# PSUM banks of the seven FFN2 products from other tiles, two partial sums moved to the q and k tiles, and a higher rank for the relu chain of the last pass

## The chip, the core and the metric

One core of a Trainium2 chip runs the whole program. The metric is the device time in microseconds of one execution. Three executions of the kernel before took 696.64, 698.77 and 699.04 us; the median is 698.77 us. A profiled execution, from which every duration below is read, took 701.44 us.

## The reference

Three layers follow each other, all in float32, on 4 x 576 = 2304 tokens of width 512:

```
s = (q @ k.T) / 8, masked to the 64 keys that end at the query      # 8 heads of 64
x = softmax(s) @ v                                                  # 2304 x 512
h = maximum(x @ w_in, 0)                                            # 512 -> 2048   (FFN1)
x = (h * h) @ w_out                                                 # 2048 -> 512
h = x @ w2_in                                                       # 512 -> 1024   (FFN2)
solu = h * softmax(h)
ln = (solu - mean) / sqrt(var + 1e-6) * g_ln
out = ln @ w2_out                                                   # 1024 -> 512
```

The weights arrive as float64 bit patterns and are turned into float32 on the core. FFN1 and FFN2 are computed with each operand split into a high part (the matrix engine's rounded float32) and a rest, in three products per pair of operands (`TERMS`).

## The kernel before

**A planner sets the order.** The kernel doesn't issue instructions directly. It calls `add(engine, us, rank, function, after, take, give, port)` for every step, with an estimated duration, a rank and the slots (buffers, PSUM banks) that the step takes and gives back. `Plan.run` then picks, again and again, the step that can start first by its own estimates (the lower rank wins a tie) and in the end emits all steps in the order of their planned starts. The order on each engine is thus fixed before the program runs; waits between engines are semaphores that the framework derives from who writes and reads which tile. `port=True` makes the planner keep a VectorE step and a GpSimd step from being planned at the same time; nothing on the chip enforces it.

**FFN1** runs in five passes of 8, 6, 8, 6 and 8 blocks of 64 tokens (`ffn`, 512 or 384 columns). In a pass each of 16 weight chunks `kk` takes 12 matrix products into a `ps_h` bank (L538), then the chain relu on ScalarE (L544), square on ScalarE (L548, the high part `g`), exact square on GpSimd (L551), rest on VectorE (L554), then 12 products into `ps_y` (L567). Attention for the next pass (`attention`, units of two blocks) is ranked between; `attention_of(t)` spreads its units over the pass before.

**The conversion of w2** (`assembled`, `operands`, `weights`) is ranked into the last pass: each 128x512 weight block is loaded, scaled on ScalarE (L219), completed by three VectorE steps (L223, L228, L233), and split into high part (ScalarE) and rest (VectorE: L278 for w2_in, L254 for w2_out). L286 forms differences of w2_in blocks.

**FFN2** treats two tiles of 128 tokens at a time (`pair2`, nine pairs, n = 0 to 8). Its 2x2 block product is done with seven products instead of eight; each is 6 matrix instructions of 512 columns (L735), into four banks called a, b, c and d. In order: A11 into a, S2 into b, S3 into d, S1 into c, then A12 added to a, A22 added to d, S4 added to c. Between them ScalarE and VectorE take the sums out: `p1` = a (L741, `keep1`), `u2` = b + p1 (L745), `u3` = d + u2 (L749), c22 = c + u3 (L760), c11 = a (L757), c21 = d + u2 (L763), c12 = c + u2 (L766). Banks a and b are two tiles of `ps_a`; banks c and d are the two halves of one two-bank tile of `ps_b`. `p1`, `u2` and `u3` are `wm` buffers, which the weight conversion uses too.

**Behind each pair** (`behind`, once per tile): maximum (L807), exp, solu (L818), centring, squares, transposes into `ps_t` (L835), high part on ScalarE (L841) and rest on VectorE (L845) of the transposed rows, 24 products with w2_out into a `ps_a` bank (L852), scaling and store.

Of the kernel before, what the change touches and what calls it, by code (L numbers as in the profile page):

```python
# [8 lines left out]
F32 = mybir.dt.float32  # L9
# [9 lines left out]
P = 128  # L19
# [5 lines left out]
class Plan:  # L25
# [14 lines left out]
    def add(self, eng, us, rank, fn, after=(), take=(), give=(), port=False, late=0.0, at=0.0):  # L40
        t = dict(eng=eng, us=us, rank=rank, fn=fn, after=[a for a in after if a], take=take, give=give, port=port, late=late, at=at,
                 start=None, n=len(self.tasks))
        self.tasks.append(t)
        return t
# [52 lines left out]
def kernel(  # L97
# [20 lines left out]
    NT, DM = out.shape  # L118
# [12 lines left out]
    HALF, LAST = len(FIRSTS), len(PASSES) - 1  # L131
# [9 lines left out]
    ps_b = ctx.enter_context(tc.tile_pool(name="ps_b", bufs=2, space=PSUM))  # L141
# [42 lines left out]
    with ExitStack() as c1:  # L184
# [344 lines left out]
        def ffn(t, n0, n1, kk, rank, done):  # L529
# [41 lines left out]
            in_of[t, kk] = i  # L571
            if kk == KF - 1:
                x_free.setdefault(t, []).append(i)
            r = add("ACT", N / 1200 + 0.11, rank, relu, [i], take=["r"], give=["a"])
            s = add("ACT", N / 1200 + 0.11, rank, square, [r], take=["g"])
            e = add("POOL", N / 600 + 0.19, rank, exact, [s], port=True)
            e = add("DVE", N / 960 + 0.07, rank, rest, [e], port=True, give=["r"])
            first = kk == 0 and n0 == 0

            before = [p for k, p in out_of.items() if k[0] == t and (last or k[1:3] == (0, 0))]  # L580
# [27 lines left out]
        CHUNKS = (16.27, 26.54, 25.57)  # L608
        V0, LATER, OUT = 3.12, 52.7, 4.55
        LEAD = 14.41  # L610
        UNIT = (1.68, 2.12, 15.1, 22.97)
        for n, (kind, kk) in enumerate((kind, kk) for kk in range(KF) for kind in "ab"):
            weights(kind, kk, LOADS[n] if n < len(LOADS) else PAIR0 + PAIR * n / 2 - 2)
# [6 lines left out]
            attention(n, rank)  # L620

        def attention_of(t):
            lo = begin[t - 1] + LATER * (t == 1)
            hi = begin[t] - 10
            n = PASSES[t] // 2
            for i in range(n):
                attention(starts[t] // 2 + i, lo + i * (hi - lo) / n)
# [47 lines left out]
        def term(name):  # L675
            return raw_p.tile([P, 512], F32, tag="wm", name=name, bufs=WMB)

        ring = {}
        phase_of = {}
        M6, TURN = 6 * (512 / 2400 + 0.0135), 0.95  # L680

        def pair2(n, rank, rank_o):
# [39 lines left out]
            WHERE = {"A11": (0, 0), "A12": (0, 1), "A22": (1, 0), "S1": (2, 0), "S2": (2, 1), "S3": (3, 0), "S4": (3, 1)}  # L722

            def product(bank, x, w, begins, ends):
                if begins and bank in "ab":
                    o[bank] = ps_a.tile([P, 512], F32, tag="a", name="ps_h2")
                elif begins and "c" not in o:
                    ps = ps_b.tile([P, 2, 512], F32, tag="b", name="ps_h2")
                    o["c"], o["d"] = ps[:, 0], ps[:, 1]
                k, half = WHERE[x]  # L730
                m = 0
                for r in range(2):
                    for wi, xi in TERMS:
                        at = half * 256 + r * P
                        T.matmul(o[bank], o["xx", k][:, xi, at : at + P], w2i[w, r][:, wi, :], start=begins and m == 0,  # L735
                                 stop=m == 5, skip_group_check=True)
                        m += 1

            def keep1():
                o["p1"] = term("p1")  # L740
                S.activation(out=o["p1"], in_=o["a"], func=AF.Copy)  # L741

            def u2():
                o["u2"] = term("u2")
                V.tensor_tensor(out=o["u2"], in0=o["b"], in1=o["p1"], op=ALU.add)  # L745

            def u3():
# [30 lines left out]
            def pe(k, bank, x, w, begins, after, **kw):  # L778
                return add("PE", M6, rank + 0.01 * k, lambda: product(bank, x, w, begins, True), [*xs_, ready[w, 0], ready[w, 1], *after], **kw)

            soon = rank - 30
            p1 = pe(0, "a", "A11", "B11", True, [], take=["a"])
            e1 = add("ACT", 0.60, soon, keep1, [p1], take=["wm"])
            p6 = pe(1, "b", "S2", "T2", True, [p1], take=["a"])
            e2 = add("DVE", 0.68, soon, u2, [p6, e1], take=["wm"], give=["a", "wm"])
            p7 = pe(2, "d", "S3", "T3", True, [p6], take=["b"])
            e3 = add("DVE", 0.68, soon, u3, [p7, e2], take=["wm"])
            p5 = pe(3, "c", "S1", "T1", True, [p7])
            f22 = add("DVE", 0.68, soon, c22, [p5, e3], take=["wb"], give=["wm"])
            p2 = pe(4, "a", "A12", "B21", False, [p5, e1])  # L790
            f11 = add("ACT", 0.60, soon, c11, [p2], take=["wb"], give=["a"])
            p4 = pe(5, "d", "A22", "T4", False, [p2, e3])
            f21 = add("DVE", 0.68, soon, c21, [p4, f22])
            p3 = pe(6, "c", "S4", "B22", False, [p4, f22], give=["wb"] * 4)
            f12 = add("DVE", 0.68, soon, c12, [p3, f11, f21], give=["b", "wm"])
            phase_of[n] = [p3]

            for k, (i, _, _) in enumerate(tiles):
                behind(k, i, o, rank + LATE0 * (n == 0), rank_o + k * 2 * mm(512), [f11, f12] if k == 0 else [f21, f22])
# [1 line left out]
        def behind(k, i, p, rank, rank_o, done):  # L801
# [62 lines left out]
            a = add("DVE", 1.95, rank, solu, [a])  # L864
            a = add("ACT", 1.10, rank, centered, [a])
            r = add("ACT", 1.25, rank + 3, squares, [a], give=["wb"])
            p_ = add("PE", TURN, rank_o - 8, transposes2, [a], take=["t", "t"])
            r = add("POOL", 2.0, rank, root, [r, p_], give=["wb"])
            ls = []
            for hf in range(2):  # L870
# [17 lines left out]
        o = {}  # L888
# [57 lines left out]
```

## Time and profile before

| what | us |
|---|---|
| median of three executions | 698.77 |
| profiled execution, whole | 701.44 |
| its span, first to last instruction | 699.6 |
| TensorE busy in the span | 682.5 |
| VectorE busy | 391.2 |
| ScalarE busy | 358.9 |
| GpSimd busy | 132.3 |

The page counts as TensorE busy also the time in which a product runs at the lower clock, so that 98% is not 98% of the work rate. A 12-product step of 512 columns shows a length of 2.88 us in the timeline and the next one starts 2.72 us after it: products overlap by their drain, and the distance of starts is what one costs. In the timelines below an instruction line ends in square brackets where the engine was idle before it, with the length of that idle time and what ended it.

### The profile page before, as it was taken

To read this page: it belongs to the slowest core of one execution; us is meant where nothing else is said; L and a number is where in the kernel's file an instruction comes from. 1 tells how busy PE (TensorE), PEld (TensorE's weight loads), DVE (VectorE), ACT (ScalarE), POOL (GpSimd) and SP (SyncE) were. 2 spreads that over 40 slices of the span, in tenths; PEclk is the share of its full clock that TensorE was granted. 3 is DMA by queue.
4 is the path that set the end of the run, shared out by engine and by line. 5 is a ranking of instruction groups with operands and counts; after the bars stand their busy time and mean duration, and the time that the engine had idled before them with its cause. 6 is when DMAs were issued, how large, how long until landed. Compare 5 with 4: busy or idle time off the path is not lost.

```text
span 699.6 us, 11257 instructions
## 1 busy us (share of the span) xinstructions
PE 682.5 (98%) x4377; PEld 576.3 (82%) x4377; DVE 391.2 (56%) x737; ACT 358.9 (51%) x831; POOL 132.3 (19%) x160
## 2 busy tenths in 40 slices
PE   8999999999999999999999999989999999999997
PEld 4678778899998888888999988877778888888885
DVE  4989989633423222114333126997985577656551
ACT  5876775624445242425444234664874466445652
POOL 1023231412323121213232112320210000000000
PEclk8999999999999999999999999999999999999999
DMA  7774656051222111103110103333021110110001
GB/s 249 231 244 142 219 192 221 4 166 54 69 69 83 33 66 35 34 2 128 54 53 31 46 31 129 112 120 121 0 91 61 60 61 31 42 49 31 30 16 45
DMA packets 33253, 60.50 MB, mean 86 GB/s; under 512 B 2992, under 2 KB 14768, under 8 KB 33200
## 3 DMA queue, kind: packets, MB, share of 16 engines
q1 hardware_dynamic: 32656, 59.52, 26.0%
q8 instruction: 34, 0.56, 0.3%
q10 hardware_dynamic: 544, 0.26, 0.1%
q14 instruction: 19, 0.16, 0.1%
HBM read 50.34 MB, written 9.44 MB: 85 GB/s over the span
## 4 chain that ended last, share of the span: by engine, by line
PE 77%; DVE 12%; ACT 4%; DMA 3%; issue 2%; SPq 1%; ACTq 0%; DVEq 0%
PE ps_y L567 24%; PE ps_h L538 21%; PE ps_o L852 13%; PE ps_h L735 10%; PE ps_v L450 2%; PE ps_s L380 2%; PE ps_lt L835 2%; PE ps_p L423 2%; ACT e L395 1%; DMA wraw<-in_w_out 1%; DVE wm L233 1%; DVE wm L228 1%; PE ps_warm L893 1%; DVE g L554 1%; DVE nmax L807 1%
## 5 line engine op out<-in xcount | busy, mean ns | idle before, releaser
L567 PE MATMUL ps_y<-g,wb 128*128 128x512 f32 (+2 forms) x1008 | 214.3, 365 | 4.0 <-DVE g L554 3.9
L538 PE MATMUL ps_h<-x,wa 128*128 128x512 f32 (+2 forms) x1008 | 209.3, 361 | 1.9 <-ACT r L544 1.2
L567 PEld LDWEIGHTS ps_y<-g,wb 128*128 128x128 f32 x1008 | 177.3, 189 | 29.1 <-DVE g L554 6.2
L538 PEld LDWEIGHTS ps_h<-x,wa 128*128 128x128 f32 x1008 | 177.1, 188 | 24.2 <-ACT r L544 1.5
L551 POOL TENSOR_TENSOR r<-r 128x512 f32<-128x512 f32 (+2 forms) x84 | 83.7, 997 | 302.4 <-ACT g L548 270.6
L554 DVE TENSOR_TENSOR g<-r,g 128x512 fp32r<-128x512 f32 (+2 forms) x84 | 56.4, 673 | 130.4 <-POOL r L551 130.4
L544 ACT ACTIVATE r<-ps_h 128x512 f32<-128x512 f32 (+2 forms) x84 | 44.8, 534 | 119.8 <-PE ps_h L538 113.9
L852 PE MATMUL ps_o<-w2o,lnT 128*128 128x512 f32 x432 | 101.2, 393 | 0.7 <-ACT lnT L841 0.4
L852 PEld LDWEIGHTS ps_o<-w2o,lnT 128*128 128x128 f32 x432 | 80.3, 188 | 17.8 <-ACT lnT L841 0.7
L395 ACT ACTIVATE e<-e,nmax 128x128 f32<-128x128 f32 x112 | 43.4, 391 | 31.6 <-DVE nmax L388 31.6
L735 PE MATMUL ps_h<-w2i,xx 128*128 128x512 f32 x189 | 53.3, 390 | 0.0
L548 ACT ACTIVATE g<-r 128x512 fp32r<-128x512 f32 (+2 forms) x84 | 47.7, 569 | 7.6 <-PE ps_y L567 5.7
L405 POOL TENSOR_TENSOR e<-e,sums 128x512 f32<-128x512 f32 x28 | 31.0, 1107 | 69.3 <-DVE sums L401 68.9
L735 PEld LDWEIGHTS ps_h<-w2i,xx 128*128 128x128 f32 x189 | 35.5, 188 | 7.6
L812 ACT ACTIVATE e<-h,nmax 128x1024 f32<-128x1024 f32 x18 | 20.7, 1150 | 34.2 <-DVE nmax L807 34.2
L829 POOL TENSOR_SCALAR rstd<-rstd 128x1 f32<-128x1 f32 x18 | 4.3, 241 | 169.5 <-ACT h L826 168.9
L219 ACT ACTIVATE wm<-wraw 128x512 f32<-128x512 f32 x47 | 31.4, 672 | 7.4 <-DMA wraw<-in_w_in 4.7
L233 DVE SCALAR_TENSOR_TENSOR wm<-wraw,wm 128x512 int32<-128x512 int32 x48 | 34.2, 716 | 0.1
L228 DVE SCALAR_TENSOR_TENSOR wm<-wraw,wm 128x512 int32<-128x512 int32 x48 | 33.4, 700 | 0.1
L383 DVE SCALAR_TENSOR_TENSOR e<-ps_s,mask 128x512 f32<-128x512 f32 x28 | 18.1, 683 | 24.4 <-PE ps_s L380 24.4
L845 DVE TENSOR_TENSOR lnT<-ps_lt,lnT 128x512 fp32r<-128x512 f32 x36 | 23.1, 683 | 14.0 <-ACT lnT L841 14.0
L463 DVE TENSOR_TENSOR x<-ps_v,x 128x512 fp32r<-128x512 f32 (+1 forms) x20 | 12.7, 636 | 24.6 <-ACT x L460 24.6
(102 smaller groups left out, 743.7 us busy)
## 6 DMA issues: line engine op xcount, KB each, us to landing
wraw<-in_w_in SPq DMA_DIRECT2D x24, 512.0 KB, 3.6
wraw<-in_w_out SPq DMA_DIRECT2D x24, 512.0 KB, 4.0
vt<-in_v SPq DMA_DIRECT2D x32, 256.0 KB, 3.0
kt<-in_k SPq DMA_DIRECT2D x16, 384.0 KB, 3.7
xr<-x_dram SPq DMA_DIRECT2D x18, 256.0 KB, 3.4
out<-o SPq DMA_DIRECT2D x18, 256.0 KB, 2.0
qt<-in_q SPq DMA_DIRECT2D x16, 256.0 KB, 2.8
x_dram<-y SPq DMA_DIRECT2D x12, 256.0 KB, 2.7
```

The costliest lines, as they stand in the source:

```text
L219: S.activation(out=o["m"], in_=o["raw"][:, :, 1].bitcast(F32), func=AF.Copy, scale=REBIAS)
L228: V.scalar_tensor_tensor(out=t, in0=o["raw"][:, :, 1], scalar=-0x80000000, in1=t, op0=ALU.bitwise_and, op1=ALU.bitwise_or)
L233: V.scalar_tensor_tensor(out=t, in0=o["raw"][:, :, 0], scalar=29, in1=t, op0=ALU.logical_shift_right, op1=ALU.bitwise_or)
L395: S.activation(out=o["er"][:, a, w], in_=s, func=AF.Exp, scale=SCALE if begins else 1.0, bias=o["nmax"][:, a, w : w + 1], accum_out=o["sum ...
L538: T.matmul(ps[:, :N], wa[kk][:, wi, c * P : c * P + P], xs[t][:, xi, c, n0:n1], start=n == 0, stop=n == 3 * DC - 1)
L544: S.activation(out=o["r"], in_=o["h"][:, :N], func=AF.Relu)
L548: S.activation(out=o["g"][:, 0, :N], in_=o["r"], func=AF.Square)
L551: G.tensor_tensor(out=o["r"], in0=o["r"], in1=o["r"], op=ALU.mult)
L554: V.tensor_tensor(out=o["g"][:, 1, :N], in0=o["r"], in1=o["g"][:, 0, :N].bitcast(F32), op=ALU.subtract)
L567: T.matmul(acc[t][d][:, n0:n1], wb[kk][:, wi, d * P : d * P + P], o["g"][:, xi, :N], start=kk == 0 and n == 0 and n0 == 0, stop=last and n ...
L735: T.matmul(o[bank], o["xx", k][:, xi, at : at + P], w2i[w, r][:, wi, :], start=begins and m == 0, stop=m == 5, skip_group_check=True)
L852: T.matmul(o["o"], o["l", hf][:, xi, kk % 4, :], w2o[kk][:, wi, :], start=kk == 0 and n == 0, stop=kk == KF2 - 1 and n == 2)
```

## The change

It has five parts.

1. In `pair2`, banks a and d now come together, and banks b and c. For pairs 0 and 1 a and d are two tiles of `ps_a`, and c and b are the halves of one `ps_b` tile that is kept from pair 0 on (`kept[0]`). From pair 2 on a and d are the halves of a second kept `ps_b` tile. The same two tiles serve all later pairs.
2. `p1` and `u2` are no longer `wm` buffers: they use the SBUF space of attention's q and k tiles, one buffer each, so that they wait for the last attention unit and for the evictions of the pair before.
3. In the last pass of FFN1 the relu chain (relu, square, exact, rest) gets a rank that is 60 lower, and `exact` is no longer planned under the port rule but 0.4 us longer.
4. Attention for passes 2 to 4 starts 4 us later in the plan (`lo`).
5. The transposes of the last two tiles are ranked 24 instead of 8 ahead of their products.

```diff
-            r = add("ACT", N / 1200 + 0.11, rank, relu, [i], take=["r"], give=["a"])
-            s = add("ACT", N / 1200 + 0.11, rank, square, [r], take=["g"])
-            e = add("POOL", N / 600 + 0.19, rank, exact, [s], port=True)
-            e = add("DVE", N / 960 + 0.07, rank, rest, [e], port=True, give=["r"])
+            soon = rank - SOON * (t == LAST)
+            r = add("ACT", N / 1200 + 0.11, soon, relu, [i], take=["r"], give=["a"])
+            s = add("ACT", N / 1200 + 0.11, soon, square, [r], take=["g"])
+            e = add("POOL", N / 600 + 0.19 + 0.4 * (t == LAST), soon, exact, [s], port=t != LAST)
+            e = add("DVE", N / 960 + 0.07, soon, rest, [e], port=True, give=["r"])
...
+        SOON = 60
...
-            lo = begin[t - 1] + LATER * (t == 1)
+            lo = begin[t - 1] + (LATER if t == 1 else 4)
...
-                if begins and bank in "ab":
+                if begins and n < 2 and bank in "ad":
                     o[bank] = ps_a.tile([P, 512], F32, tag="a", name="ps_h2")
-                elif begins and "c" not in o:
-                    ps = ps_b.tile([P, 2, 512], F32, tag="b", name="ps_h2")
-                    o["c"], o["d"] = ps[:, 0], ps[:, 1]
+                elif begins and bank not in o:
+                    if n in (0, 2):
+                        kept.append(ps_b.tile([P, 2, 512], F32, tag="b", name="ps_h2"))
+                    o.update(c=kept[0][:, 0], b=kept[0][:, 1])
+                    if n > 1:
+                        o.update(a=kept[1][:, 0], d=kept[1][:, 1])
...
-                o["p1"] = term("p1")
+                o["p1"] = at_p.tile([P, 512], F32, tag="q", name="p1", bufs=1)
...
-                o["u2"] = term("u2")
+                o["u2"] = at_p.tile([P, 512], F32, tag="k", name="u2", bufs=1)
...
+            p1 = pe(0, "a", "A11", "B11", True, free if n > 1 else [], take=["a"] if n < 2 else ["b"] * (n == 2))
+            e1 = add("ACT", 0.60, soon, keep1, [p1, *gone_by, *free])
+            p6 = pe(1, "b", "S2", "T2", True, [p1, *free], take=["b"] * (n == 0))
+            e2 = add("DVE", 0.68, soon, u2, [p6, e1, *gone_by, *free])
+            p7 = pe(2, "d", "S3", "T3", True, [p6, *free], take=["a"] * (n < 2))
...
-            p_ = add("PE", TURN, rank_o - 8, transposes2, [a], take=["t", "t"])
+            p_ = add("PE", TURN, rank_o - (8 if i < NT // P - 2 else 24), transposes2, [a], take=["t", "t"])
```

Where it moves instructions, first on TensorE where the last pass of FFN1 meets pair 0 (`ps_h` with a number is a bank of the seven products, `x24` are two steps in a row). Before, the last FFN1 steps and the first products of the pair:

```order
L567 MATMUL ps_y<-g,wb 128x512 x24
L538 MATMUL ps_h<-x,wa 128x512 x12
L567 MATMUL ps_y<-g,wb 128x512 x12
L538 MATMUL ps_h<-x,wa 128x512 x12
L735 MATMUL ps_h_4654<-w2x,xx 128x512 x3
L735 MATMUL ps_h_4654<-w2i,xx 128x512 x3
L567 MATMUL ps_y<-g,wb 128x512 x12
L735 MATMUL ps_h_4700<-w2v,xx 128x512 x3
L735 MATMUL ps_h_4700<-w2i,xx 128x512 x3
L567 MATMUL ps_y<-g,wb 128x512 x12
```

Now:

```order
L567 MATMUL ps_y<-g,wb 128x512 x12
L538 MATMUL ps_h<-x,wa 128x512 x12
L567 MATMUL ps_y<-g,wb 128x512 x12
L538 MATMUL ps_h<-x,wa 128x512 x12
L567 MATMUL ps_y<-g,wb 128x512 x12
L538 MATMUL ps_h<-x,wa 128x512 x12
L567 MATMUL ps_y<-g,wb 128x512 x12
L742 MATMUL ps_h_4724<-w2x,xx 128x512 x3
L742 MATMUL ps_h_4724<-w2i,xx 128x512 x3
L742 MATMUL ps_h_4736<-w2v,xx 128x512 x3
```

The products of pair 0, which stood between the last three steps into `ps_y`, now follow in one piece behind a strict alternation of L538 and L567; its first two products go to 4724 and 4736, and the third and fourth to 4748 and 4736.

On VectorE in the last pass (`wm` are the conversion's buffers, L554 is the end of the relu chain). Before, up to the 13th L554 of the 16 in this pass:

```order
L286 TENSOR_TENSOR wm<-wm 128x512
L278 TENSOR_TENSOR w2i<-wm,w2i 128x512
L223 TENSOR_SCALAR wm<-wm 128x512
L278 TENSOR_TENSOR w2i<-wm,w2i 128x512 x2
L228 SCALAR_TENSOR_TENSOR wm<-wraw,wm 128x512
L223 TENSOR_SCALAR wm<-wm 128x512
L233 SCALAR_TENSOR_TENSOR wm<-wraw,wm 128x512
L228 SCALAR_TENSOR_TENSOR wm<-wraw,wm 128x512
L554 TENSOR_TENSOR g<-r,g 128x512
L233 SCALAR_TENSOR_TENSOR wm<-wraw,wm 128x512
L254 TENSOR_TENSOR w2o<-wm,w2o 128x512 x2
L554 TENSOR_TENSOR g<-r,g 128x512
```

Now, up to the same one:

```order
L278 TENSOR_TENSOR w2i<-wm,w2i 128x512
L286 TENSOR_TENSOR wm<-wm 128x512
L278 TENSOR_TENSOR w2i<-wm,w2i 128x512
L286 TENSOR_TENSOR wm<-wm 128x512
L278 TENSOR_TENSOR w2i<-wm,w2i 128x512
L286 TENSOR_TENSOR wm<-wm 128x512
L554 TENSOR_TENSOR g<-r,g 128x512
L278 TENSOR_TENSOR w2i<-wm,w2i 128x512 x3
L223 TENSOR_SCALAR wm<-wm 128x512 x2
L228 SCALAR_TENSOR_TENSOR wm<-wraw,wm 128x512 x2
L233 SCALAR_TENSOR_TENSOR wm<-wraw,wm 128x512 x2
L554 TENSOR_TENSOR g<-r,g 128x512
```

The 13th L554 now stands ahead of the first w2_out steps (L254), and the 12th ahead of the last three splits of w2_in (L278).

On TensorE in pair 3, the last four of its seven products (the later pairs go the same way). Before:

```order
L735 MATMUL ps_h_5383<-w2e,xx 128x512 x3
L735 MATMUL ps_h_5383<-w2i,xx 128x512 x3
L735 MATMUL ps_h_5360<-w2x,xx 128x512 x3
L735 MATMUL ps_h_5360<-w2i,xx 128x512 x3
L735 MATMUL ps_h_5383<-w2p,xx 128x512 x3
L735 MATMUL ps_h_5383<-w2i,xx 128x512 x3
L735 MATMUL ps_h_5383<-w2x,xx 128x512 x3
L735 MATMUL ps_h_5383<-w2i,xx 128x512 x3
```

Now:

```order
L742 MATMUL ps_h_4736<-w2e,xx 128x512 x3
L742 MATMUL ps_h_4736<-w2i,xx 128x512 x3
L742 MATMUL ps_h_5105<-w2x,xx 128x512 x3
L742 MATMUL ps_h_5105<-w2i,xx 128x512 x3
L742 MATMUL ps_h_5105<-w2p,xx 128x512 x3
L742 MATMUL ps_h_5105<-w2i,xx 128x512 x3
L742 MATMUL ps_h_4736<-w2x,xx 128x512 x3
L742 MATMUL ps_h_4736<-w2i,xx 128x512 x3
```

The order of the products is the same; S1 and S4 (w2e and the last w2x) write one tile, A12 and A22 (the first w2x and w2p) the other, where before S1, A22 and S4 all wrote tile 5383.

## Rows read from the trace of the kernel before

**Rows 1.** The page: engines, busy us, share of the span, instructions.

```profile
PE 682.5 (98%) x4377; PEld 576.3 (82%) x4377; DVE 391.2 (56%) x737; ACT 358.9 (51%) x831; POOL 132.3 (19%) x160
```

**Rows 2.** Busy time by stretch; columns PE, PEld, DVE, ACT, POOL, clock, DMA, GB/s.

```profile
426.11:470.49 44.38, 42.54 (x185) 34.82 (x184) 41.77 (x65) 27.83 (x49) 10.92 (x8) 0.98 0.39 122
...
465.00:470.00 5.00, 3.16 (x12) 2.22 (x11) 4.15 (x9) 3.88 (x7) 0.00 (x0) 0.88 0.40 115
...
470.00:475.00 5.00, 5.00 (x19) 4.00 (x18) 3.67 (x6) 1.49 (x3) 1.04 (x1) 0.77 0.29 95
```

**Rows 3.** Who TensorE waited for: total us, times, longest.

```profile
PE ps_y L567 <- DVE g L554: 3.9, 4, 1.8
...
PE ps_h L735 <- DVE h L760: 1.8, 5, 1.2
```

**Rows 4.** TensorE in order of time, 432 to 532 us: start, us, instruction, idle before.

```profile
434.37 2.88 PE L567 MATMUL ps_y<-g,wb 128*128 128x512 f32 x12
...
464.29 0.84 PE L735 MATMUL ps_h<-w2x,xx 128*128 128x512 f32 x3
...
467.88 4.29 PE L567 MATMUL ps_y<-g,wb 128*128 128x512 f32 x11 [1.84 <-DVE g L554]
...
481.70 0.97 PE L735 MATMUL ps_h<-w2p,xx 128*128 128x512 f32 x3 [1.23 <-DVE h L760]
...
484.56 2.88 PE L567 MATMUL ps_y<-g,wb 128*128 128x512 f32 x12
...
487.28 5.60 PE L538 MATMUL ps_h<-x,wa 128*128 128x512 f32 x24
...
517.75 5.73 PE L852 MATMUL ps_o<-w2o,lnT 128*128 128x512 f32 x24
```

**Rows 5.** Weight loads of the products, pairs 3 and 8 (first and last of six).

```profile
553.81 0.53 PEld L735 LDWEIGHTS ps_h<-w2p,xx 128*128 128x128 f32 x3 [0.57 <-DVE h L760]
...
665.81 0.64 PEld L735 LDWEIGHTS ps_h<-w2i,xx 128*128 128x128 f32 x3
...
667.02 0.53 PEld L735 LDWEIGHTS ps_h<-w2p,xx 128*128 128x128 f32 x3 [0.57 <-DVE h L760]
...
669.66 1.02 PEld L835 LDWEIGHTS ps_lt<-ident,e 128*128 128x128 f32 x8
```

**Rows 6.** Every engine in order of time: evictions of pair 8.

```profile
662.91 0.69 DVE L745 TENSOR_TENSOR u<-ps_h,p 128x512 f32<-128x512 f32 x1 [1.13 <-PE ps_h L735]
...
665.56 0.69 DVE L749 TENSOR_TENSOR u<-ps_h,u 128x512 f32<-128x512 f32 x1 [1.96 <-PE ps_h L735]
...
666.28 0.69 DVE L760 TENSOR_TENSOR h<-ps_h,u 128x512 f32<-128x512 f32 x1
```

**Rows 7.** VectorE and GpSimd in the last pass of FFN1.

```profile
426.11 0.69 DVE L554 TENSOR_TENSOR g<-r,g 128x512 fp32r<-128x512 f32 x1 [3.78 <-POOL r L551]
...
460.83 1.56 POOL L551 TENSOR_TENSOR r<-r 128x512 f32<-128x512 f32 x1 [5.16 <-ACT g L548]
...
461.40 1.53 DVE L286 TENSOR_TENSOR wm<-wm 128x512 f32<-128x512 f32 x1
...
467.14 0.68 DVE L554 TENSOR_TENSOR g<-r,g 128x512 fp32r<-128x512 f32 x1
...
470.49 1.54 DVE L554 TENSOR_TENSOR g<-r,g 128x512 fp32r<-128x512 f32 x1
```

**Rows 8.** TensorE at the start of pass 3.

```profile
321.18 2.35 PE L538 MATMUL ps_h<-x,wa 128*128 128x384 f32 x12 [1.22 <-ACT r L544]
```

**Rows 9.** TensorE at the end of the program.

```profile
669.89 1.03 PE L835 MATMUL ps_lt<-ident,e 128*128 128x128 f32 x8
...
670.68 11.14 PE L852 MATMUL ps_o<-w2o,lnT 128*128 128x512 f32 x48
...
683.14 0.50 PE L852 MATMUL ps_o<-w2o,lnT 128*128 128x512 f32 x1 [0.44 <-ACT lnT L841]
...
687.28 8.42 PE L852 MATMUL ps_o<-w2o,lnT 128*128 128x512 f32 x36
```

More of the change, by code (lines that the diff above doesn't have):

```diff
@@ L678 @@
         ring = {}
-        phase_of = {}
+        kept = []
+        phase_of, read_of = {}, {}
+        gone_by = [p_after[len(UNITS) - 1]]
         M6, TURN = 6 * (512 / 2400 + 0.0135), 0.95
@@ L781, in pair2 @@
             soon = rank - 30
[L782 to L786, printed above, removed]
+            free = read_of.get(n - 1, [])
+            p1 = pe(0, "a", "A11", "B11", True, free if n > 1 else [], take=["a"] if n < 2 else ["b"] * (n == 2))
[3 more added lines that the diff above has]
+            p7 = pe(2, "d", "S3", "T3", True, [p6, *free], take=["a"] * (n < 2))
+            p5 = pe(3, "c", "S1", "T1", True, [p7])
             e3 = add("DVE", 0.68, soon, u3, [p7, e2], take=["wm"])
-            p5 = pe(3, "c", "S1", "T1", True, [p7])
             f22 = add("DVE", 0.68, soon, c22, [p5, e3], take=["wb"], give=["wm"])
             p2 = pe(4, "a", "A12", "B21", False, [p5, e1])
-            f11 = add("ACT", 0.60, soon, c11, [p2], take=["wb"], give=["a"])
+            f11 = add("ACT", 0.60, soon, c11, [p2], take=["wb"], give=["a"] * (n < 2))
             p4 = pe(5, "d", "A22", "T4", False, [p2, e3])
-            f21 = add("DVE", 0.68, soon, c21, [p4, f22])
+            f21 = add("DVE", 0.68, soon, c21, [p4, f22], give=["a"] * (n < 2))
             p3 = pe(6, "c", "S4", "B22", False, [p4, f22], give=["wb"] * 4)
-            f12 = add("DVE", 0.68, soon, c12, [p3, f11, f21], give=["b", "wm"])
-            phase_of[n] = [p3]
+            f12 = add("DVE", 0.68, soon, c12, [p3, f11, f21])
+            phase_of[n], read_of[n] = [p3], [f11, f12, f21]
             for k, (i, _, _) in enumerate(tiles):
```

## The prediction

> **What bounds the kernel now.** I read the page's engine list first: TensorE is busy 682.5 of 699.6 us, the next engine VectorE 391.2 [rows 1]. So only time that TensorE stands still or runs slowly can be won. The table of stretches comes next, to find that time: the clock is below 1 only in two stretches after the start, at 465 to 475 us [rows 2]. The list of waits says for whom TensorE stands: for L554, the end of the relu chain, 3.9 us, and for L760, an eviction of the seven products, 1.8 us [rows 3]. Last, TensorE's timeline between 434 and 518 us [rows 4] shows where.
>
> One unit is needed. The step at 487.28 starts 2.72 us after the one at 484.56 [rows 4], so a 512-column instruction costs 2.72 / 12 = 0.2267 us, and a block of FFN1, one L538 and one L567, 5.44 us. What a stretch takes beyond its instructions is loss, also where the list of waits shows none.
>
> - From 464.29 to 484.56 TensorE does pair 0 (42 instructions) and two L567 (24): 66 x 0.2267 = 14.96 us in 20.27. Loss 5.31: the wait of 1.84 for L554, the slow clock right behind it, and the wait of 1.23 at A22 [rows 4].
> - From 484.56 to 517.75 it does 126 such instructions and two sets of eight transposes of 0.79 us (669.89 to 670.68 [rows 9]): 28.56 + 1.58 = 30.14 us in 33.19. Loss 3.05.
> - Six pairs (3 to 8) wait at the weight load of A22, the w2p product. In pair 8 the starts at 665.81 and 669.66 lie five steps apart; at 0.68 us a step (three instructions) that is 3.40 in 3.85 us. Loss 0.45, six times 2.7 [rows 5].
> - At the start of pass 3 there is a wait of 1.22 us [rows 8]. At the end, 96 instructions and two sets of transposes are 23.34 us; from 670.68 to 687.28 + 36 x 0.2267 = 695.44 they take 24.76. Loss 1.42 [rows 9].
>
> Together 13.7 us of loss that this change can touch.
>
> **The change part by part.** *Banks.* In pair 8 u3 starts at 665.56, after VectorE had been idle 1.96 us, until S1's product ended [rows 6]. u3 needs only bank d, which S3 had finished two steps earlier; but S1 writes c, the other half of the same tile. c22 follows at 666.28 and ends at 666.97, and A22, which needs only u3, starts at 667.02, since it writes the tile that c22 reads. Now d lies in one tile with a, c with b. u3 then waits for S3 alone. The new sharing adds other waits: S1 for u2's reading of b, A12 for u3's reading of d, S3 for ScalarE's copy of a. Counted back from 665.81 in steps of 0.68, the first weight loads of S3, S1 and A12 were at 662.41, 663.77 and 665.13. u2 ran from 662.91 to 663.60 [rows 6], 0.17 us before S1's load. u3 would follow S3 as u2 follows S2, 0.50 us behind the first load of the next product: 664.27 to 664.96, 0.17 before A12's. These margins hold as long as VectorE is free at that moment, as it was (1.13 us idle before u2). A miss would cost what it is late. c11 now waits for A22 on ScalarE, and c21 for c11; only the maximum stands behind them. Of 2.7 I take 2.4, since 0.17 us is little; bounds 0 and 2.7.
>
> The Trainium skill, page "PSUM — Partial Sum Buffer", section "PSUM bank collisions raise a hardware error", says that two engines at different banks don't disturb each other. By that rule sharing a tile costs nothing on the chip and the 0.45 us would have another cause and stay; the trace's idle time of u3, until a product into another bank ended, speaks for the program's semaphores instead.
>
> *The relu chain.* VectorE is nearly full from the 6th to the 13th L554, 426.11 to 470.49: 41.77 of 44.38 us busy [rows 2, 7]. The 12th L554 ran only at 467.14, though its GpSimd square had ended at 462.39 [rows 7]: 4.75 us of conversion stood ahead of it, and L567 waited. With the new rank the 12th stands ahead of three splits, the 13th ahead of w2_out. TensorE alternates strictly, so the 13th L567 would start at 434.37 (the 7th) + 6 x 5.44 = 467.0 without waits. Can VectorE follow? The 41.8 us of work were 64 instructions, or, without seven meetings with GpSimd of 0.85 us (below), 0.56 us for one. Now it is 63: two w2_out splits fewer, one rest of the x operands more, so 41.2. The 13th L554 starts at 467.3 at the earliest, and with half of the old 2.6 us of idle time, for loads and ScalarE, at 468.6; its L567 then at 469.3, some 2.3 us late in all, spread over seven steps. Then pair 0 follows: A22 would start 2.72 + 6.8 = 9.5 us later, at 478.8. On VectorE 18 instructions run from the 13th L554 to u3, with one meeting 18 x 0.56 + 0.85 = 10.9 us: done at 479.5. A22 waits 0.7. Pair 0 ends at 482.2 against 484.56: gain 2.35. The ends: 0 if the queue is late by 2.35 more, 5.31 if nothing waits.
>
> *GpSimd without the port rule.* It is only the plan that changes; the two engines met before too: L286 took 1.53 instead of 0.68 us at 461.40, beside the square that began at 460.83 [rows 7]. That 0.85 is in the 41.2. The plan no longer counts it, so VectorE will run later than planned.
>
> The Trainium skill, page "SBUF — State Buffer", section "Who interferes with whom", says that a VectorE step with two inputs in SBUF and a GpSimd step that reads SBUF exclude each other, and the later one stands until the other has ended. By it one meeting could cost up to the square's 1.56 us instead of 0.85; over seven steps that would be 5.0 us more and no gain in this stretch.
>
> *From pair 0 to the first L852.* Counted the same way, the 15th and 16th L554 come some 11 and 13 us after pair 0's end; their L567, behind 54 and 66 instructions, 12.2 and 15.0 after it. Pair 1's last products and the transposes have a margin near 1 us, on a ScalarE that is as full. I keep a third of the loss: gain 2.0, bounds 0 and 3.05.
>
> *Attention 4 us later.* At the start of pass 3 three L538 of 384 columns stood in a row behind the scores, and the third had to wait for a relu behind eight exps [rows 8]. Now one L567 stands between; I estimate 0.4 us left, gain 0.8. Ends: the full 1.22, or as much again lost at another of the eleven moved units, -1.2.
>
> *Last transposes.* They come 12 instructions earlier, so that their rows are converted beside the products of the tile before; two such waits in the end stretch become one of about 0.5 us behind ScalarE's squares. Gain 0.9, bounds 0 and 1.42.
>
> *p1 and u2 in other buffers* remove no work and wait for nothing later than the evictions of the pair before, which end over 10 us earlier, under 48 products: zero.
>
> Sum: 2.4 + 2.35 + 2.0 + 0.8 + 0.9 = 8.45 us. The profiled execution took 701.44, so 693.0; it lies 2.67 above the median of 698.77. Taken from the median, 690.3.
>
> **Rivals.** *VectorE stays the bound (18%).* It is 94% busy in the last pass before and its work is the same; if ScalarE's waits keep all its old idle time, pair 0 and pair 1 end when they did. Left are 2.4 + 0.8 + 0.9 = 4.1: 694.7. Against it: 4.75 us of queue stood before a result that TensorE waited for, and less urgent work can go behind.
>
> *The products wait on (12%).* One of the new shared waits is late by as much as the old one in each pair: 8.45 - 2.4 = 6.05: 692.7. Margins of 0.17 us speak for it, the idle times of rows 6 against it.
>
> *Slower (5%).* The strict alternation has no spare L538 to fill with. If at each L567 of the last pass the chain is late as at 467.88, TensorE loses 1.84 plus the slow clock behind: granted 0.88 and 0.77 of full speed over two times 5 us [rows 2], where 1 is the 2.4 GHz level and its half 1.2, so 0.12 x 5 + 0.23 x 5 = 1.75 us. That is 3.6 for one. Elsewhere 6.1 are won and 5.31 of old loss goes, so it decides from 3.2 such waits on; five give 18.0 - 11.4 = +6.6: 705.4. For it: each block needs some 6 us of VectorE in 5.44 us of TensorE. Against: VectorE enters with a lead of over 2 us, and waits of 1.2 us brought no lower clock.
>
> *The sum as forecast: 65%*, with its own range 687.2 to 693.2.
>
> **How the numbers follow.** A measurement of this kernel can tell 0.5%, 3.5 us: faster is below 695.3, slower above 702.3. The forecast and the second rival are faster, 77%; of the first rival (694.7, give or take 2) two thirds, 12%, of which I move 6% to no change for gains in the forecast that come out smaller. Faster 0.83, same 0.12, slower 0.05. For the range I go down to 685.8, nearly all of the 13.7, and up to 695.8, past the first rival.
>
> **What would show it.** Right: no idle time at A22's weight load in pairs 3 to 8, and pairs 22.2 instead of 22.65 us apart; u3 right behind S3; the 12th and 13th L554 each next after its square; the clock at 1 from 460 to 480; pair 0 done near 482 us. Wrong: the 13th L567 later than 471, long waits for L554 at every block, a new wait at S1 or S3, or new waits of L538 for a relu in passes 1 to 3.

## The result and the profile after

The changed kernel takes 689.5 us (median of four runs, 688.96 to 690.26), the kernel before 698.9 beside it: ratio 0.9872, 95% interval 0.9847 to 0.9897. The forecast was 690.3. The profiled execution took 688.96, its span is 687.2. The page's lines that answer to [rows 1], and TensorE's clock by slice:

```profile
PE 675.0 (98%) x4377; PEld 573.7 (83%) x4377; DVE 392.5 (57%) x737; ACT 359.1 (52%) x831; POOL 136.0 (20%) x160
PEclk9999999999999999999999999999999999999999
```

VectorE has as much to do as before (392.5 against 391.2 us), TensorE is busy 7.5 us less. The stretches that answer to [rows 2] (columns as there):

```profile
425.00:471.10 46.10, 44.67 (x192) 35.42 (x191) 43.36 (x68) 29.05 (x51) 13.66 (x8) 1.00 0.43 139
465.00:470.00 5.00, 4.23 (x20) 3.49 (x19) 4.96 (x8) 3.17 (x6) 1.08 (x2) 1.00 0.48 193
470.00:475.00 5.00, 5.00 (x24) 4.13 (x22) 5.00 (x10) 4.40 (x8) 0.00 (x0) 1.00 0.69 213
```

The clock stays at 1.00, and from 465 to 475 us VectorE is busy 9.96 of 10 us. TensorE's waits (us in total, times, longest), for [rows 3], and three rows of its timeline, for [rows 4]:

```profile
PE ps_y L567 <- DVE g L554: 2.9, 4, 0.9
PE ps_h L742 <- DVE u L756: 0.5, 1, 0.5
```

```profile
465.79 2.79 PE L567 MATMUL ps_y<-g,wb 128*128 128x512 f32 x11 [0.77 <-DVE g L554]
...
475.85 0.96 PE L742 MATMUL ps_h<-w2p,xx 128*128 128x512 f32 x3 [0.47 <-DVE u L756]
...
478.77 2.88 PE L567 MATMUL ps_y<-g,wb 128*128 128x512 f32 x12
```

L742 is now the line of the seven products. The first row is the 13th L567, the second A22 of pair 0, the third the step behind pair 0. In pair 8, for [rows 5, 6], the weight loads from A12's second group to S4, and VectorE's u2, u3, c22 and c21:

```profile
655.01 0.64 PEld L742 LDWEIGHTS ps_h<-w2i,xx 128*128 128x128 f32 x3
655.69 0.64 PEld L742 LDWEIGHTS ps_h<-w2p,xx 128*128 128x128 f32 x3
656.37 0.64 PEld L742 LDWEIGHTS ps_h<-w2i,xx 128*128 128x128 f32 x3
657.05 0.64 PEld L742 LDWEIGHTS ps_h<-w2x,xx 128*128 128x128 f32 x3
```

```profile
652.10 0.69 DVE L752 TENSOR_TENSOR u<-ps_h,p 128x512 f32<-128x512 f32 x1 [1.14 <-PE ps_h L742]
653.39 0.69 DVE L756 TENSOR_TENSOR u<-ps_h,u 128x512 f32<-128x512 f32 x1 [0.60 <-PE ps_h L742]
654.75 0.69 DVE L767 TENSOR_TENSOR h<-ps_h,u 128x512 f32<-128x512 f32 x1 [0.67 <-PE ps_h L742]
658.10 0.69 DVE L770 TENSOR_TENSOR h<-ps_h,u 128x512 f32<-128x512 f32 x1 [2.66 <-ACT h L764]
```

The loads stand 0.68 us apart without a gap, A22's (w2p) too, and u3 runs one product earlier than before, right behind S3.

Where the time went, stretch by stretch of the two profiled executions (starts of the same steps subtracted):

| stretch | before | after | gain | forecast |
|---|---|---|---|---|
| L567 near 100 us to the 7th L567 of the last pass | 332.43 | 331.47 | 0.96 | 0.8 |
| 7th to 14th L567, pair 0 among them | 50.19 | 48.60 | 1.59 | 2.35 |
| from there over 192 products and four sets of transposes | 50.27 | 47.54 | 2.73 | 2.0 |
| from there to the last pair's end | 135.85 | 133.12 | 2.73 | 2.4 |
| last pair's end to the last 36 products | 16.60 | 15.39 | 1.21 | 0.9 |

The gains sum to 9.2 us, forecast 8.45; the medians differ by 9.4. Another 3.2 us of the two traces' difference lie ahead of 100 us, where the change moves nothing: the execution of before that was profiled had a lower clock there (its page gives the clock of the first slice as 8 tenths, the page of after as 9), and with 701.44 us it was 2.7 above its median. So the table reads like a forecast that came true term by term. The experiments say otherwise.

The medians also hold a share of TensorE's clock. The kernel before was executed 57 times beside the experiments: the 13 executions with a mean granted clock of 1.000 have a median of 696.3 us, the 33 with 0.998 or less one of 699.3. All eight timed executions of the changed kernel have 1.000, with a median of 689.3. By these numbers I estimate that some 2.4 us of the gain are a clock that no longer fell, and some 7.0 are left at the same clock.

### The profile page after: what moved, and what is told of

Read it like the earlier page. It is cut to its first block, busy times and chain, and to the rows that moved or that the text cites. A ratio compares the mean times of both kernels' runs of the same rounds, so it can differ in the third digit from the quotient of the medians.

```text
span 687.2 us, 11252 instructions
## 1 busy us (share of the span) xinstructions
PE 675.0 (98%) x4377; PEld 573.7 (83%) x4377; DVE 392.5 (57%) x737; ACT 359.1 (52%) x831; POOL 136.0 (20%) x160
## 4 chain that ended last, share of the span: by engine, by line
PE 82%; DVE 8%; ACT 3%; DMA 3%; issue 2%; POOL 1%; SPq 1%; ACTq 0%; POOLq 0%
PE ps_y L567 24%; PE ps_h L538 23%; PE ps_o L860 14%; PE ps_h L742 11%; PE ps_v L450 2%; PE ps_lt L843 2%; PE ps_s L380 2%; ACT e L395 2%; PE ps_p L423 2%; DMA wraw<-in_w_out 1%; PE ps_warm L901 1%; POOL r L551 1%; DVE wm L233 1%; DVE wm L228 1%; DVE g L554 1%
## 5 line engine op out<-in xcount | busy, mean ns | idle before, releaser
L567 PE MATMUL ps_y<-g,wb 128*128 128x512 f32 (+2 forms) x1008 | 214.1, 363 | 3.1 <-DVE g L554 2.9
L538 PE MATMUL ps_h<-x,wa 128*128 128x512 f32 (+2 forms) x1008 | 209.6, 360 | 0.6 <-DVE x L463 0.5
L567 PEld LDWEIGHTS ps_y<-g,wb 128*128 128x128 f32 x1008 | 176.3, 188 | 27.9 <-DVE g L554 5.9
L538 PEld LDWEIGHTS ps_h<-x,wa 128*128 128x128 f32 x1008 | 177.0, 188 | 23.4 <-issue 1.4
L551 POOL TENSOR_TENSOR r<-r 128x512 f32<-128x512 f32 (+2 forms) x84 | 87.7, 1045 | 290.3 <-ACT g L548 281.7
L554 DVE TENSOR_TENSOR g<-r,g 128x512 fp32r<-128x512 f32 (+2 forms) x84 | 57.0, 679 | 118.6 <-POOL r L551 118.6
L860 PE MATMUL ps_o<-w2o,lnT 128*128 128x512 f32 x432 | 101.2, 392 | 0.2 <-DVE lnT L853 0.2
L860 PEld LDWEIGHTS ps_o<-w2o,lnT 128*128 128x128 f32 x432 | 80.3, 188 | 16.7 <-DVE lnT L853 0.6
L742 PE MATMUL ps_h<-w2i,xx 128*128 128x512 f32 x189 | 53.1, 389 | 0.0
L742 PEld LDWEIGHTS ps_h<-w2i,xx 128*128 128x128 f32 x189 | 35.5, 188 | 7.5
L820 ACT ACTIVATE e<-h,nmax 128x1024 f32<-128x1024 f32 x18 | 20.7, 1150 | 16.6 <-DVE nmax L815 14.9
L764 ACT ACTIVATE h<-ps_h 128x512 f32<-128x512 f32 x9 | 5.4, 595 | 43.2 <-PE ps_h L742 43.2
```

Source lines behind the costliest of these rows:

```text
L538: T.matmul(ps[:, :N], wa[kk][:, wi, c * P : c * P + P], xs[t][:, xi, c, n0:n1], start=n == 0, stop=n == 3 * DC - 1)
L551: G.tensor_tensor(out=o["r"], in0=o["r"], in1=o["r"], op=ALU.mult)
L554: V.tensor_tensor(out=o["g"][:, 1, :N], in0=o["r"], in1=o["g"][:, 0, :N].bitcast(F32), op=ALU.subtract)
L567: T.matmul(acc[t][d][:, n0:n1], wb[kk][:, wi, d * P : d * P + P], o["g"][:, xi, :N], start=kk == 0 and n == 0 and n0 == 0, stop=last and n ...
L860: T.matmul(o["o"], o["l", hf][:, xi, kk % 4, :], w2o[kk][:, wi, :], start=kk == 0 and n == 0, stop=kk == KF2 - 1 and n == 2)
```

## The experiments

Ten more kernels were timed in three sets, each beside the kernel before (medians 698.4 to 698.8); the changed kernel and the one with the port rule kept were timed twice. "Middle" is the distance in the profiled execution from the first 512-column L567 of the last pass to the last product of pair 8 (its last three matrix instructions), which leaves the start and the end out; before it is 401.73 to 669.20.

| kernel | median us | ratio, 95% interval | middle us |
|---|---|---|---|
| before | 698.8 | 1 | 267.5 |
| changed | 689.5 | 0.9872, 0.9847 to 0.9897 | 260.4 |
| banks and buffers alone | 690.1 | 0.9882, 0.9853 to 0.9912 | 258.7 |
| banks alone | 693.1 | 0.9907, 0.9877 to 0.9938 | 261.2 |
| buffers alone | 697.1 | 0.9978, 0.9959 to 0.9997 | 266.8 |
| relu rank alone | 698.8 | 1.0001, 0.9982 to 1.0020 | 267.4 |
| attention and transposes alone | 695.9 | 0.9961, 0.9942 to 0.9980 | 265.9 |
| changed without banks and buffers | 695.9 | 0.9967, 0.9950 to 0.9984 | 266.4 |
| changed without the relu rank | 688.1 | 0.9841, 0.9815 to 0.9867 | 258.8 |
| changed, port rule kept | 687.7 | 0.9841, 0.9816 to 0.9867 | 257.8 |
| banks and buffers alone, S2 put back | 691.8 | 0.9910, 0.9888 to 0.9932 | 259.1 |
| changed, other tile partners | 691.8 | 0.9901, 0.9866 to 0.9935 | 263.2 |

**One part at a time.** My theory was the forecast's: semaphores go by tile and cost six waits of 0.45 us, and the relu chain stood behind conversion.

Banks and buffers alone (parts 1 and 2; parts 3 to 5 undone):

```
-            soon = rank - SOON * (t == LAST)
+            soon = rank
...
-            lo = begin[t - 1] + (LATER if t == 1 else 4)
+            lo = begin[t - 1] + LATER * (t == 1)
...
```

> The kernel before with the new banks of the seven products and the new buffers of p1 and u2 alone. Theory (the program's semaphores go by tile, and c22's reading of c's tile held up A22): the idle time at A22's weight load in pairs 3 to 8 is gone, each of these pairs takes about 0.45 us less, 2.4 to 2.7 us in all, so about 696.4 beside 698.9; the transition around pair 0 keeps its loss of about 5 us. Rival (the 0.45 us have another cause, so that sharing a tile costs nothing): the waits stay, 698.9.

Measured 690.1: 8.6 us, not 2.4. The pairs from 3 on do take 22.19 instead of 22.65 us (distances of the copy of a), as expected; the other 6 us come in the transition (from the last pass of FFN1 to pair 3), where I had given the banks nothing.

The rank alone (part 3 on the kernel before, so that the port rule of the squares goes as well):

> The kernel before with the last pass's relu chain ranked above the weight conversion (and its GpSimd square planned 0.4 us longer and without the port rule) alone. Theory (a result that TensorE waits for stood behind conversion in VectorE's queue): the stretch from the 7th to the 14th L567 shortens by about 1.6 to 2.4 us and the one behind it, to the first products of the last stage, by 2 to 3, about 4.5 in all, 694.4; the six waits of 0.45 us at A22 stay. Rival (VectorE's sum of work sets the end of this stretch, in whatever order): nothing is gained, 698.9.

The rival's number: 698.8. The theory of the chain's place in the queue was right in its first step, and part 3 as it stands was worth nothing. TensorE's waits of this kernel (L737 is the products' line, L762 is c22):

```profile
PE ps_y L567 <- DVE g L554: 2.3, 5, 0.7
PE ps_h L737 <- DVE h L762: 1.9, 1, 1.9
```

The long wait of 1.84 at L567 [rows 4] is gone, but A22 of pair 0 waits 1.86 us for c22, which reads the other half of its tile (the last 1.2 us of it; until then u3, which A22 needs, is late too). What the rank won is lost at the next place. This edit drops the port rule as well, and two squares take 2.93 and 2.83 us in its trace; what that costs is told below. The rank with the rule kept was not run on the old tiles.

Attention and last transposes alone (parts 4 and 5):

> The kernel before with the attention units 4 us later and the last transposes ranked earlier alone. Theory: the wait of 1.22 us at the start of pass 3 goes and most of the loss of 1.4 us behind the last pair goes, 1.7 to 2.2 us, so about 697.0 beside 698.9; nothing else moves. Rival (each wait removed comes back as another): 698.9.

Measured 695.9, 2.9 us less (the interval of the ratio is 1.4 to 4.1 us). In the traces, which can't be added up to the medians, 1.1 us are gained between 100 us and the last pass and 0.7 behind the last pair, as forecast. Another 1.6 in the middle are no work of the edit that I can name: the waits there are the same (1.82 for L554, 1.23 for c22), but the granted clock stays at 1.00 behind them, where it was 0.88 and 0.77 in [rows 2], 1.75 us by the forecast's count.

**Why the banks gain 8.6.** Two ideas: the banks let S2 of pair 0 go ahead of the 12th L567, since S2's bank no longer comes from the tiles of FFN1's products; or p1 and u2 no longer hold conversion buffers.

Buffers alone:

```
-                o["p1"] = term("p1")
+                o["p1"] = at_p.tile([P, 512], F32, tag="q", name="p1", bufs=1)
...
-                o["u2"] = term("u2")
+                o["u2"] = at_p.tile([P, 512], F32, tag="k", name="u2", bufs=1)
...
```

> The kernel before with p1 and u2 in the buffers of q and k alone; the banks as before. It is to say why the banks and buffers together gained 8.7 us and not 2.4. Theory of the banks (S2's bank no longer comes from the two tiles that FFN1's products use, so that S2 stands ahead of the 13th L567 and fills the wait for it): here S2 still stands behind the 13th L567, so the transition loses as before: 698.8, at most 1 us less. Rival (p1 and u2 leave the ring of four conversion buffers, and conversion no longer waits for one): most of the 6 us of the transition comes here, about 693.

Measured 697.1: 1.5 us, near the theory of the banks, though not zero.

Banks alone:

> The kernel before with the new banks alone; p1 and u2 stay in the ring of conversion buffers. Theory of the banks: 690 to 691, nearly all of what banks and buffers gained together. Rival (the buffers): only the waits in pairs 3 to 8 go, 2.4 us: 696.4.

Measured 693.1, between the two: 5.5 us. The difference to banks and buffers together stands at one place in the traces: at the first L860 TensorE waits 1.8 us for the rest of the transposed rows, and the granted clock from 505 to 525 us is 0.91; with the buffers that wait is 0.88 and the clock 1.00. So the banks are the main part, and the buffers add 1.5 alone and some 2 to 3 with the new banks (1.7 by the two ratios, 3.0 by the medians, which are of two sets; those intervals overlap).

S2 put back behind the 12th L567 (the 13th by the earlier expectations' count), with banks and buffers new and parts 3 to 5 undone:

```
-            p6 = pe(1, "b", "S2", "T2", True, [p1, *free], ...
+            p6 = pe(1, "b", "S2", "T2", True, [p1, *free] + [out_of[LAST, 0, 11, PASSES[LAST] * BLK]] * (n == 0), ...
```

> The kernel before with the new banks and the new buffers, as in the first experiment, and S2 of pair 0 tied behind the 12th L567 of the last pass (called the 13th in an earlier expectation), where it stands in the kernel before. Theory (S2 in front of that L567 gives VectorE the time that TensorE would wait): the wait for L554 of about 1.8 us and the low clock behind it come back, some 3 to 4 us of the 8.7 are lost, about 693.5. Rival (the tiles alone do it: A22 of pair 0 and what follows is no longer held by c22): no more than 1 us is lost, 690 to 691.

Measured 691.8, between the two numbers, and 1.6 us above banks and buffers alone with overlapping intervals: the times don't decide. The trace, which is of the fastest of its six executions, speaks for the rival: the middle is 259.1, only 0.3 us longer than with S2 in front. The wait at that L567 came back, the low clock did not (1.00 behind it), and what follows loses nothing. The other five executions are 1.1 to 1.9 us longer, and which of them lost clock at this place isn't on record. So S2's place explains little of the transition's gain in the traces.

```profile
465.10 2.81 PE L567 MATMUL ps_y<-g,wb 128*128 128x512 f32 x11 [1.83 <-DVE g L554]
```

What differs from before is VectorE. In the kernel before, the evictions u2, u3 and c21 of pair 0, and S4's first product:

```profile
473.70 0.69 DVE L745 TENSOR_TENSOR u<-ps_h,p 128x512 f32<-128x512 f32 x1 [1.33 <-PE ps_h L735]
479.15 0.69 DVE L749 TENSOR_TENSOR u<-ps_h,u 128x512 f32<-128x512 f32 x1 [0.82 <-PE ps_h L735]
484.76 0.69 DVE L763 TENSOR_TENSOR h<-ps_h,u 128x512 f32<-128x512 f32 x1 [2.05 <-PE ps_h L735]
```

```profile
483.20 0.84 PE L735 MATMUL ps_h<-w2x,xx 128*128 128x512 f32 x3
```

Of products, c21 (the last of the three) needs A22 alone, whose last product is followed by S4's first at 483.20, but S4 writes the other half of its tile and was issued before it; c21 starts when S4 has ended, and the next step on TensorE has begun at 484.56 [rows 4]. So about 1.4 of its 2.05 us are the tile's. With the new tiles (banks and buffers alone) its wait is 0.28:

```profile
476.08 0.69 DVE L770 TENSOR_TENSOR h<-ps_h,u 128x512 f32<-128x512 f32 x1 [0.28 <-PE ps_h L742]
```

While VectorE, the fullest engine of this stretch, stands there, the conversion and the chains queued behind it come later. VectorE's busy time from 465 to 485 us (third engine column), first before, then the rank alone, then attention and transposes alone, then banks and buffers, then S2 put back:

```profile
465.00:485.00 20.00, 16.93 (x66) 13.16 (x65) 14.91 (x26) 10.49 (x17) 1.04 (x1) 0.91 0.43 132
```

```profile
465.00:485.00 20.00, 17.40 (x69) 13.62 (x68) 15.59 (x27) 12.64 (x21) 2.21 (x2) 0.91 0.39 132
```

```profile
465.00:485.00 20.00, 18.70 (x80) 14.96 (x81) 16.30 (x29) 10.71 (x18) 1.04 (x1) 1.00 0.49 156
```

```profile
465.00:485.00 20.00, 20.00 (x88) 16.37 (x89) 19.43 (x33) 13.85 (x25) 1.76 (x2) 1.00 0.49 156
```

```profile
465.00:485.00 20.00, 19.90 (x87) 16.31 (x88) 19.04 (x32) 12.88 (x22) 1.04 (x1) 1.00 0.46 156
```

With the old tiles it works 14.9 to 16.9 of 20 us (the most in the changed kernel with the old banks), also with the new rank, where c21 alone waits 4.09 us, about half of them for A22's own products, which ran at the low clock, and half for S4:

```profile
485.73 0.69 DVE L765 TENSOR_TENSOR h<-ps_h,u 128x512 f32<-128x512 f32 x1 [4.09 <-PE ps_h L737]
```

With the new tiles it works 18.5 and more in every kernel, wherever S2 stands. Buffers alone belong to the first kind (14.92 busy, the same three waits of 1.33, 0.82 and 2.04).

Not all of the transition's 6 us is the tiles' work, though: in the trace of before, 1.6 us go to the clock that fell behind the 12th L567. The kernel with parts 4 and 5 alone and the one with S2 put back can be compared without that: old and new tiles, the same order up to there, the same wait (1.82 and 1.83), the clock at 1.00 behind it. From the first 512-column L567 on, pair 0 ends 1.55 us earlier with the new tiles (478.74 - 398.96 against 480.29 - 398.95), the copy of a in pair 3 comes 4.28 earlier, and the last conversion step of VectorE (L254) stands 97.5 us behind it in place of 100.6. So the transition gains some 4.3 us by the new banks and buffers at the same clock: 1.55 at A22, the rest behind pair 0, where the conversion is done earlier. That the freed time of VectorE is what shortens that rest is argued from these rows; no run separates it.

**Is it the tile?** The changed kernel, same instructions in the same order on every engine, from pair 2 on with other partners:

```
-                    o.update(c=kept[0][:, 0], b=kept[0][:, 1])
+                    o.update(c=kept[0][:, 0], **{"b" if n < 2 else "a": kept[0][:, 1]})
-                        o.update(a=kept[1][:, 0], d=kept[1][:, 1])
+                        o.update(b=kept[1][:, 0], d=kept[1][:, 1])
```

> The changed kernel with the same instructions in the same order on every engine, and from pair 2 on other partners for the banks: c shares its tile with a, and b with d. Theory (waits go by tile): S3, which writes d, now waits for u2's reading of b, which ends 1.2 us behind S3's present first weight load, and A12, which writes a, waits for c22's reading of c, 1.2 us more; 2.4 us in each of pairs 2 to 8, 16.7 in all: about 706 beside 689.5. Rival (two banks of one tile don't hinder each other, and the old 0.45 us came from somewhere else): 689.5.

Measured 691.8: 2.3 us more, not 16.7. The pairs grow from 22.19 to 22.53. Pair 8's u2 and c22, and the weight loads of A22 and S4:

```profile
656.63 0.69 DVE L752 TENSOR_TENSOR u<-ps_h,p 128x512 f32<-128x512 f32 x1 [2.50 <-PE ps_h L742]
...
659.28 0.69 DVE L767 TENSOR_TENSOR h<-ps_h,u 128x512 f32<-128x512 f32 x1 [1.23 <-PE ps_h L742]
```

```profile
658.86 0.64 PEld L742 LDWEIGHTS ps_h<-w2p,xx 128*128 128x128 f32 x3
659.54 0.64 PEld L742 LDWEIGHTS ps_h<-w2i,xx 128*128 128x128 f32 x3
660.66 0.53 PEld L742 LDWEIGHTS ps_h<-w2x,xx 128*128 128x128 f32 x3 [0.48 <-ACT h L764]
```

The tile does decide, since nothing else was changed: u2 now runs behind S3 (d, its new partner) and c22 behind A12. But I had the direction wrong. S3 is issued before u2, so u2 waits for S3, not S3 for u2; only S4's load waits (for the copy c11, issued before it, which itself waited for c22, a reader of the same tile): 660.66 in place of 660.22, 0.44 us late there. What is issued first is waited for.

**The rank and the port rule.** Without the rank, parts 1, 2, 4 and 5 alone:

> The changed kernel without the new rank of the relu chain and with its port rule back: banks, buffers, attention units and last transposes alone. Theory (the rank gained nothing by itself, and with the banks it costs what S2 in front of the 13th L567 already gave): the two gains measured alone, 8.7 of the banks and 2.7 of attention and transposes, add up: 687.4, faster than the changed kernel by about 2. Rival (the forecast: the rank brings 4.4 us in the transition): 693.9.

Measured 688.1: the gains of banks and buffers (8.6) and of parts 4 and 5 (2.9) nearly add up, and the rank brings none of its 4.4 us.

The changed kernel with the port rule kept for the last pass's square:

```
-            e = add("POOL", N / 600 + 0.19 + 0.4 * (t == LAST), soon, exact, [s], port=t != LAST)
+            e = add("POOL", N / 600 + 0.19, soon, exact, [s], port=True)
```

> The changed kernel with the port rule kept for the last pass's GpSimd square (and its planned 0.4 us more left out); the rank stays. Theory (the rank itself costs, since with it TensorE alternates strictly between L538 and L567 and each L567 meets the chain's latency): no better than the changed kernel, 689.5 to 691. Rival (the squares that now run beside VectorE's two-input steps cost, seven of them 1.44 to 2.94 us long): about 687.5.

Measured 687.7: the rival. Since the two kernels had been timed in different sets, both once more side by side:

> The changed kernel once more, to be timed beside the one with the port rule kept: 689.5 by its own earlier runs.

> The changed kernel with the port rule kept once more, beside the changed kernel on the same chip. Theory (the squares beside VectorE's two-input steps cost some 2.7 us between the start of the last pass and the last product, as the two traces show): about 2 faster, 687.5. Rival (the difference of the first two timings is scatter): the same, 689.5.

Measured 689.3 (688.99 to 689.57; 0.9874, 0.9849 to 0.9898) for the changed kernel and 686.5 (686.26 to 687.82; 0.9838, 0.9812 to 0.9863) with the rule kept. The ratios' intervals overlap, but no run of the one lies within 1.1 us of a run of the other, and the middles of the two are 260.4 and 257.8. The squares show the likely cause. GpSimd in the changed kernel, then with the rule kept (its second timing):

```profile
443.66 2.94 POOL L551 TENSOR_TENSOR r<-r 128x512 f32<-128x512 f32 x1 [4.60 <-ACT g L548]
448.87 1.28 POOL L551 TENSOR_TENSOR r<-r 128x512 f32<-128x512 f32 x1 [2.28 <-ACT g L548]
455.42 1.44 POOL L551 TENSOR_TENSOR r<-r 128x512 f32<-128x512 f32 x1 [5.27 <-DVE wm L286]
462.18 2.83 POOL L551 TENSOR_TENSOR r<-r 128x512 f32<-128x512 f32 x1 [5.31 <-ACT g L548]
```

```profile
448.27 1.17 POOL L551 TENSOR_TENSOR r<-r 128x512 f32<-128x512 f32 x1 [3.46 <-ACT g L548]
454.09 1.04 POOL L551 TENSOR_TENSOR r<-r 128x512 f32<-128x512 f32 x1 [4.64 <-ACT g L548]
459.53 1.04 POOL L551 TENSOR_TENSOR r<-r 128x512 f32<-128x512 f32 x1 [4.40 <-ACT g L548]
465.28 1.62 POOL L551 TENSOR_TENSOR r<-r 128x512 f32<-128x512 f32 x1 [4.71 <-ACT g L548]
```

Two squares of the changed kernel take 2.8 to 2.9 us instead of 1.04, so their chains reach L554 and TensorE later. Pair 0's first product comes 70.9 us after the first 512-column L567 in it (468.41 - 397.53), and 68.0 with the rule kept (466.81 - 398.81, its first timing): the whole difference is made by then. On VectorE of the changed kernel the square of 443.66 looks so:

```profile
443.81 0.68 DVE L233 SCALAR_TENSOR_TENSOR wm<-wraw,wm 128x512 int32<-128x512 int32 x1
444.42 0.68 DVE L228 SCALAR_TENSOR_TENSOR wm<-wraw,wm 128x512 int32<-128x512 int32 x1
445.02 0.68 DVE L724 TENSOR_TENSOR xx<-xs,xx 128x512 fp32r<-128x512 f32 x1
446.63 0.69 DVE L554 TENSOR_TENSOR g<-r,g 128x512 fp32r<-128x512 f32 x1 [0.94 <-POOL r L551]
```

It ended at 446.60, 0.90 us after VectorE's step of 445.02 had ended at 445.70: nearly its whole own time lies behind VectorE's run, and VectorE then stood 0.94 us for it. The second long square ends 0.91 us behind such a run. Two things limit this. The edit changes the planned order on VectorE as well (L554 stands at other places), and no run parts the order from the squares. And the rule doesn't exclude such meetings: the kernel before, which has it, shows one of 3.01 us too, at a place where TensorE had a second L538 to go on with and didn't wait:

```profile
442.06 3.01 POOL L551 TENSOR_TENSOR r<-r 128x512 f32<-128x512 f32 x1 [4.20 <-DVE wm L286]
```

```profile
437.09 5.60 PE L538 MATMUL ps_h<-x,wa 128*128 128x512 f32 x24
```

The kernel with the rule kept is the fastest of the study; the rank with the rule kept is worth 1.0 us of the middle beside the kernel without the rank (257.8 against 258.8), too little for the medians to tell.

The complement of the first experiment, the changed kernel with the old banks and buffers:

> The changed kernel with the banks and buffers of before: the rank of the relu chain, the attention units and the last transposes are as changed. Theory (banks and buffers carry the gain, the rank by itself nothing): only the 2.7 of attention and transposes are left, about 696. Rival (the rank is worth its 4.4 us once the other parts stand beside it): about 691.7.

Measured 695.9, the theory's number: what parts 4 and 5 give alone. A22 of pair 0 waits 2.5 us for c22 in it.

## Why the prediction was right, and where it was not

The total came out (690.3 forecast, 689.5 measured) because two terms were wrong by about as much in opposite directions: that the sum fits is luck.

- **Banks** (2.4 us, bounds 0 and 2.7). The mechanism was right, and so was the size in pairs 3 to 8; the margins of 0.17 us held. The term was mis-sized, since it counted those six pairs only: banks and buffers alone gain 8.6, 6 of them in the transition (4.3 at the same clock). The rows for it were at hand: the 1.23 us at A22 of pair 0 [rows 4] names c22, the same release as in pair 8, and I booked it under the relu chain. What I didn't look up were VectorE's own waits at pair 0's evictions.
- **Relu chain** (2.35, and 2.0 up to the first L852). This step failed. The chain did wait behind conversion, and the signs that I named came: the 13th L567 starts its second instruction at 465.79, with the 4.20 us by which this execution is ahead at the 7th L567 469.99 (forecast 469.3), A22 waits 0.47 (0.7), pair 0 ends at 482.97 (482.2). But without the rank pair 0 ends earlier still, at 480.14 by the same count and with no wait at A22 (banks and buffers alone, 2.90 us ahead at the 7th L567). Part 3 alone is worth 0 (a gain of -1.4 to +1.3 us), and in the changed kernel nothing; the rank with the port rule kept is worth some 1.0 there and is untested with the old tiles. Of the rivals, "VectorE stays the bound" was right for this edit: the new order moved a wait within a full queue, while VectorE's idle time, which the tiles made, was there to win. Its time (694.7) was wrong, because the banks' share was.
- **GpSimd without the port rule** ("only the plan that changes"). Wrong: dropping the rule cost 1.8 to 2.8 us. I took 0.85 us for a meeting from one row [rows 7], a square that met one VectorE step; two squares now met a run of them and took 1.8 and 1.9 us more. The rule that I weighed and left, that the later of the two stands until the other has ended (the Trainium skill, "SBUF — State Buffer", "Who interferes with whom"), agrees with the square of 443.66 in that it stood, and ended 0.90 us behind the run; but it stood over three steps of VectorE in a row, where I had priced one. The meetings of 1.5 us don't decide.
- **p1 and u2** (zero). Not zero: 1.5 us alone (0.2 to 2.9), some 2 to 3 with the new banks. I looked at what they wait for, not at the conversion buffers that they give back.
- **Attention and last transposes** (0.8 and 0.9). Right within what the traces tell: 1.0 and 1.2 in the changed kernel's trace, 1.1 and 0.7 in the trace of the two alone. The median of the two alone gains 2.9; in the trace another 1.6 is a clock that didn't fall.

What stays open: why the clock fell behind some of the waits and not behind others (below), what the rank is worth with the port rule kept on the old tiles, and the buffers' effect, which is located, not explained.

## What to carry to other kernels

A wait that is named once by the page in the steady state is to be looked for everywhere that the same code runs, above all where another engine is full: the same tile partner cost 0.45 us a pair in the steady pairs and, with the buffers, some 4 us in the transition, where it held up the fullest engine's queue and not only TensorE. Count that engine's own idle time, and what released it, before re-ranking its queue: here a better order won nothing while the head of the queue stood idle. And when several edits go in together, agreement of the signs with the forecast doesn't say which edit made them; each must be run alone.

## What was not expected of the hardware

- The same wait of TensorE leaves different clocks. A granted clock of 1.00 is the 2.4 GHz level throughout; a smaller number is a stretch with some time at 1.2 GHz. Behind 1.84 us at the 12th L567 the granted clock was 0.88 and 0.77 in two stretches of 5 us [rows 2], and 0.66 in one with the buffers alone; behind 1.82 and 1.83 us at the same instruction (parts 4 and 5 alone, S2 put back) it was 1.00. Behind 1.86 us at A22 it was 0.66 (the rank alone, 480 to 485), behind 2.5 us at A22 1.00 (old banks in the changed kernel). A forecast shouldn't book the low clock as certain.
- GpSimd's square of 128x512, 1.04 us by itself, took 2.83 to 3.01 us beside runs of VectorE steps with two inputs, while single meetings took VectorE's step from 0.68 to 1.53 us and the square from 1.04 to some 1.5.
